# Block sums spread by DMA, expert 0's w2 in two loads, and one more x transposed by DMA, in a fused sparse-attention and routing kernel

## The chip, the cores and the metric

The kernel runs on one core of a Trainium2 chip. The metric is device time in microseconds (us). Before the change the median of three runs is 668.64 us (668.12 to 669.35). Five engines take part: TensorE (PE; its weight loads are listed as PEld), VectorE (DVE), ScalarE (ACT), GpSimd (POOL) and SyncE (SP). SP only issues DMAs; POOL mostly does. Each engine works through its own instructions in the order in which they were written, so an instruction that waits holds up everything behind it on that engine.

## The reference

The computation is a sparse attention whose output, with all heads side by side, is the input of a dense mixture of experts. Shapes: q, k and v are 4 batches x 8 heads x 768 positions x 64; the experts' input x is 3072 x 512; there are 8 experts with 1024 hidden units.

```python
k_sum = k.reshape(B, H, nb, 32, D).max(axis=3)      # 24 blocks of 32 keys
v_sum = v.reshape(B, H, nb, 32, D).mean(axis=3)
scores_l = where(|i - j| < 16, scale * q @ k.T, -1e9)
scores_s = scale * q @ k_sum.T + log(32)
a = softmax(concat(scores_l, scores_s))             # one softmax over both
attn = a @ concat(v, v_sum)
x = attn with heads side by side                    # (3072, 512)
P = exp(x @ w_gate - max)
repeat 8 times: P /= row sums; P /= column sums; P *= N / E
out = sum over e of P[:, e] * (relu(x @ w1[e]) @ w2[e])
```

Each query therefore sees its 31 nearest keys and, for every block of 32 keys, one summary key (the maximum) with one summary value (the mean).

## The kernel before

**Pairs.** Two heads are handled together as a "pair"; there are 16 pairs, four to a batch (`PB = 4`, `NP = 16`). For a pair, a chunk of 128 queries (there are `G = 6`) is multiplied with its 128 keys plus 16 on each side. Pairs 0 to 3 (batch 0) are done in two halves, with special code that brings the first results early. Pairs 4 to 15 are "whole" pairs, and most of the change concerns them.

**A whole pair** goes through these steps. k, q and v are loaded by POOL's DMAs, which cast from f32 to bf16 (`load_qk` L268, `load_v` L285). k and q are transposed to put the head dimension on partitions: on TensorE (`tr` L292) for pairs below `BY_DMA = 12`, by a DMA that SP issues (`tr_dma` L325) from there on. DVE takes the block maxima of k. TensorE sums v over blocks (`block_sums` L349), and DVE writes the sums into `V_e` (`block_out` L358). TensorE makes scores (`scores` L380), ACT exponentiates them, DVE masks them. `values` (L427) multiplies with v and, in a second product per chunk, with `V_e`; DVE normalizes (`normalize` L529); the result is transposed into `xT` on TensorE (`to_xT` L544, line L548) and copied out by DVE or ACT (`x_out` L551). For pairs at or above `X_BY_DMA = 12`, except the last of a batch, SP issues a DMA that transposes instead (`x_dma` L556).

**V_e** is a value buffer with one row of slots per chunk, `[128, G, 2 * 65]` in bf16. Its rows 0 to 63 hold the block sums of the pair's two heads, the same for every chunk. Its rows 64 to 127 hold the few neighbouring values on either side of each chunk, brought there by four small DMAs (`near_values` L369), issued by SP for pairs below 12 and by POOL above. In the kernel before, DVE writes the sums to chunk 0 and then copies them to the five others (L365). There are `NE = 2` such buffers, used in turn, and pair i cannot write its buffer until the value products of pair i - 2 are through. POOL fills in the constants (`value_constants` L692).

**Expert 0 in between.** While the attention runs, TensorE fills the time between its steps with expert 0: x of a batch is cut in two halves of 384 tokens, and each half takes 8 hidden products of four matmuls (`hidden0` L594, line L209) and 3 output products in two parts of four matmuls each (`project0` L605, line L214). Part 0 reads the first half of w2's rows, part 1 the second. The router's products (`logits`, line L568) need the whole of a batch's x. Experts 1 to 7 follow as one long run, in a form with fewer products per block (L762 and L813); this run is not touched.

**The order.** All of this is registered as units with a cost, dependencies and a priority, and a planner (`Plan.order` L58) plays it through with these costs and writes the instructions out, engine by engine, in the order that it found. A unit's `lag` is what the planner adds after its end before others may start; for a load it stands for the time to landing (`load` L860). The costs and lags decide only the order. What an instruction really waits for comes from what it reads and writes. POOL's loads form one chain: pair 0's q and so on down to v of pair 4 (L1051), then expert 0's w2 (L1052), then the constants of the `V_e` and `E_e` buffers (L1053 to L1055), then the loads of pair 5 onward. Up to `NQ = 6` pairs are loaded ahead.

Of the kernel before, what the change touches and what calls it, by code (L numbers as in the profile page):

```python
# [10 lines left out]
BF16 = mybir.dt.bfloat16  # L11
F16 = mybir.dt.float16
# [116 lines left out]
def kernel(  # L129
# [10 lines left out]
    nc = tc.nc  # L140
# [19 lines left out]
    BY_DMA = 12  # L160
    X_BY_DMA = 12
    WHOLE = 12
# [30 lines left out]

    def load_w2(e):
        w2s[e] = wpool.tile([128, KF, DM], F16, tag="w2", name="w2")
        nc.gpsimd.dma_start(out=w2s[e][:], in_=moe_w2[e].rearrange("(fk p) d -> p fk d", p=128))

# [21 lines left out]
    NB = PB  # L219
    NE = 2  # L220
    NS = 1
    NA = 3
    stage = ExitStack()
    with tc.manual_schedule():
# [20 lines left out]

        E_e = [attn.tile([128, G, 128], BF16, name=f"Ee{i}") for i in range(NE)]
        V_e = [attn.tile([128, G, 2 * VD], BF16, name=f"Ve{i}") for i in range(NE)]

# [109 lines left out]
        def block_out(i):  # L358
            vs = at.pop(("vs", i))[0:64, :].rearrange("p (j d) -> p j d", j=2)
            dst = V_s[i][0:64, :] if i < PB else V_e[i % NE][0:64, 0, :]  # L360
            nc.vector.tensor_tensor(out=dst.rearrange("p (j x) -> p j x", j=2)[:, :, 0:D], in0=vs,
                                    in1=own_n[:].to_broadcast([64, 2, D]), op=ALU.mult)
            if i >= PB:
                ve = V_e[i % NE]
                nc.vector.tensor_copy(out=ve[0:64, 1:G, :],  # L365
                                      in_=ve[0:64, 0:1, :].to_broadcast([64, G - 1, 2 * VD]))


        def near_values(i):  # L369

            sv, ve = v_x[i % NQ], V_e[i % NE]
            eng = nc.sync if i < BY_DMA else nc.gpsimd
            for j in range(2):
                c0, q0 = VD * j, 64 + 32 * j
                eng.dma_start(out=ve[q0 + W:q0 + 2 * W, 1:G, c0:c0 + VD],
                              in_=sv[128 - W:128, j, 0:G - 1, :])
                eng.dma_start(out=ve[q0:q0 + W, 0:G - 1, c0:c0 + VD],
                              in_=sv[0:W, j, 1:G, :])
# [48 lines left out]
        def values(i, h):  # L427
            sv, ee, ve, em = v_x[i % NQ], E_e[i % NE], V_e[i % NE], at["em", i]
            av = at["av", i, h] = bank("a", "av")
            for cc in range(HG):  # L430
                c, o = HG * h + cc, cc * 2 * VD
                for j in range(2):
                    nc.tensor.matmul(av[:, o + j * VD:o + (j + 1) * VD],  # L433
                                     lhsT=em[:, j, c, :], rhs=sv[:, j, c, :],
                                     start=(cc == 0 and j == 0), stop=False,
                                     skip_group_check=True)
            for cc in range(HG):
                c, o = HG * h + cc, cc * 2 * VD
                nc.tensor.matmul(av[:, o:o + 2 * VD], lhsT=ee[:, c, :], rhs=ve[:, c, :],  # L439
                                 start=False, stop=True, skip_group_check=True)  # L440
# [418 lines left out]

        def load(key, fn, issue, us, deps=()):  # L860
            last[0] = add("POOL", issue, fn, [last[0], *deps])
            last[1] = add("DMA", us, None, [add("RING", 0, None, [last[0]], lag=1.4 if last[1] else 0.9), last[1]], 100.0)
            U[key] = add("LAND", 0, None, [last[1]], lag=0.9)

        def load_pair(i, parts="kqv"):
            old = i - NQ
            for c in parts:
                if c == "v":
                    load(("v", i), lambda: load_v(i), 1.05, 1.85 if i < PB else 1.6,
                         [U.get(("A", old, 1)), U.get(("near", old))])  # L870
                elif i < PB and c in "qr":
                    h = "qr".index(c)
                    load(("q", i, h), lambda h=h: load_qk(i, 1, h), 0.65, 0.65)
                else:
                    z = "kq".index(c)
                    load((c, i), lambda z=z: load_qk(i, z), 0.75 if i < PB else 1.65,
                         1.2 if i < PB else 1.4, [U.get(("tr", old, z)), U.get(("tr", old, 2))])

        def pair_start(i, prio):
# [18 lines left out]
            if i >= PB:  # L898
                U["km", i] = add("DVE", 0.23, lambda: key_max_split(i), [U["ks", i]] + war_q[2:], prio)
            buf = Buffer("a")  # L900
            U["vs", i] = add("PE", 0.4, lambda: block_sums(i),
                             [U["v", i]] + ([U.get(("A", i - NE, 1)), U["vc", i % NE]] if i >= PB else []), prio + 0.01, opens=[buf])
            sc = add("DVE", 0.25, lambda: summary_constants(i), [], prio - 1.0) if 0 < i < PB else None
            U["Vs", i] = add("DVE", 0.28 if i < PB else 0.7, lambda: block_out(i), [U["vs", i], sc],
                             prio + 0.01, uses=[buf])
# [36 lines left out]
        def pair_whole(i, prio):  # L942
            U["near", i] = add("SP" if i < BY_DMA else "POOL", 2.4 if i < BY_DMA else 3.0, lambda: near_values(i),
                               [U["v", i], U.get(("A", i - NE, 1)), U["vc", i % NE]], prio, lag=5.0 if i < BY_DMA else 3.5)
            x1 = []
# [24 lines left out]
            for h in range(2):  # L970
                buf = Buffer("a")
                U["A", i, h] = add("PE", 0.4, lambda h=h: values(i, h),
                                   [U["mk", i, h], U["ed", i], U["sx", i, h], U["Vs", i], U["near", i]],
                                   prio, opens=[buf])
# [13 lines left out]
        def expert0(t0, xs):  # L988
            key, n = t0, len(halves)
            halves.append(key)  # L990
            pr = 1000.0 + n
            w = [U["w1", n] for n in range(4)]
            evac, old = [], [U.get(("pj", halves[n - 2], c)) for c in range(HG)] if n >= 2 else []
# [15 lines left out]
            for c in range(HG):  # L1009
                buf = Buffer("m")  # L1010
                p0 = add("PE", 0.88, lambda c=c: project0(key, c, 0), evac[0:4] + [U["w2"]],
                         pr + 0.1 + c * 0.02, opens=[buf])
                p1 = add("PE", 0.88, lambda c=c: project0(key, c, 1), evac[4:8] + [p0],
                         pr + 0.11 + c * 0.02, uses=[buf])
# [31 lines left out]
        for n in range(4):  # L1046
            load(("w1", n), lambda n=n: load_w1(0, n, 4), 0.85, 1.25)
            if n == 1:
                for i in range(PB):
                    load_pair(i, "r")  # L1050
        load_pair(PB, "kqv")  # L1051
        load("w2", lambda: load_w2(0), 0.85, 4.0)  # L1052
        for n in range(NE):  # L1053
            U["vc", n] = last[0] = add("POOL", 1.2, lambda n=n: value_constants(n), [last[0]])
            U["ec", n] = last[0] = add("POOL", 0.7, lambda n=n: edge_constants(n), [last[0]])  # L1055
# [36 lines left out]
        def transposed():  # L1092
# [4 lines left out]
            if X_BY_DMA < NP:  # L1097
                nc.gpsimd.tensor_copy(out=warm[:, 4:5], in_=xT[0:32, PB - 2, (B - 1) * S:(B - 1) * S + 1])
            ve = V_e[(NP - 1) % NE]
            for j in range(2):  # L1100
                nc.gpsimd.tensor_copy(out=warm[:, 2 + j:3 + j],
                                      in_=ve[64 + 32 * j:96 + 32 * j, G - 2, VD * j:VD * j + 1])

        last[0] = add("POOL", 0.3, transposed, [last[0], U["near", NP - 1]] + [U["kT", NP - 1, z] for z in range(2)]
                      + [U["x", i] for i in range(X_BY_DMA, NP - 1)])
# [211 lines left out]
```

The softmax here doesn't subtract the row's maximum and nothing guards it: scores larger than these inputs give would overflow.

## Time and profile before

| what | us |
|---|---|
| median of three runs | 668.64 |
| the profiled execution | 668.44 |
| its span, first instruction to last | 666.70 |
| TensorE busy in the span | 657.9 |
| DVE busy | 549.2 |
| ACT busy | 410.5 |
| POOL busy | 198.3 |
| DVE copies of block sums to five chunks (L365), 12 of 0.483 | 5.8 |
| TensorE transposes of x (L548) in the whole span | 78 instructions |
| w2 of expert 0, from issue to landing | 10.49 |

The profile is one execution on the chip. A row for a group of instructions names the line, the engine, the operation, and what it writes and reads ("out<-in"), followed by the count and the times. A timeline row starts with the start in us from the span's start and the duration; a bracket at the end gives the engine's idle time just before and what ended it. A row for DMA issues gives the count, the size of one and the median time from issue to landing. The granted TensorE clock is full throughout the span.

### The profile page before, as it was taken

Reading aid. Unit: us, or ns where it says so; the run is one execution under the profiler, and the core shown is the slowest. Engines: PE = TensorE matmul, PEld = TensorE weight load, DVE = VectorE, ACT = ScalarE, POOL = GpSimd, SP = SyncE. Lnnn points to the kernel's source line nnn. Section 1 sums busy time; section 2 is a strip of 40 time slices with the busy share of each in tenths; the row PEclk is TensorE's granted clock in tenths of the full one; section 3 lists DMA queues with packets and bytes.
Section 4 is the critical chain, followed back from the end, with each engine's and each line's share of the span. In section 5 each row is a group of like instructions: output and inputs, shape, how many; then the busy total and the mean of one; then the engine's idle time right before and its main releaser. Section 6 shows DMA issues by size and latency. Waiting matters only on the chain.

```text
span 666.7 us, 13260 instructions
## 1 busy us (share of the span) xinstructions
PE 657.9 (99%) x5132; PEld 434.0 (65%) x5132; DVE 549.2 (82%) x1035; ACT 410.5 (62%) x768; POOL 198.3 (30%) x256
## 2 busy tenths in 40 slices
PE   8999999999999999999999999999999999999996
PEld 4656665555676666666666666666666666666665
DVE  7889978799989787888789887888778877988776
ACT  6767766555986566556565665656665656556652
POOL 8899622100132222222221222222122213222123
PEclk9999999999999999999999999999999999999999
DMA  9999992700863647473654656373837465334656
GB/s 168 165 149 145 132 88 43 127 0 1 137 112 64 117 75 116 79 127 64 98 102 76 123 83 106 65 127 61 130 64 130 77 95 95 64 64 112 159 134 198
DMA packets 112542, 67.89 MB, mean 102 GB/s; under 512 B 77920, under 2 KB 90464, under 8 KB 112480
## 3 DMA queue, kind: packets, MB, share of 16 engines
q0 software_dynamic: 94800, 57.46, 65.7%
q1 hardware_dynamic: 17152, 9.58, 6.5%
q8 instruction: 40, 0.66, 0.4%
q14 instruction: 22, 0.18, 0.1%
q10 hardware_dynamic: 528, 0.02, 0.0%
HBM read 52.45 MB, written 6.29 MB: 88 GB/s over the span
## 4 chain that ended last, share of the span: by engine, by line
PE 94%; DMA 3%; POOL 2%; issue 0%; DVE 0%; ACT 0%; POOLq 0%; DVEq 0%
PE yps L813 22%; PE pA L762 22%; PE pY L813 17%; PE pQ L762 11%; PE yps L214 6%; PE hps L209 6%; PE pR L762 5%; DMA w<-in_moe_w_dram 3%; PE sg L345 1%; PE tkq L301 1%; PE av L433 1%; PE vs L355 1%; PE av L439 1%; POOL vx L287 1%; PE tx L548 1%; PE ss L459 1%
## 5 line engine op out<-in xcount | busy, mean ns | idle before, releaser
L813 PEld LDWEIGHTS <-h 128*128 128x128 f16 x2352 | 230.1, 98 | 89.3 <-issue 1.0
L841 POOL DMA_DIRECT2D out_acc<-y x120 | 101.5, 880 | 372.0 <-ACT y L837 97.8
L837 ACT ACTIVATE y<-pY,P_sb 128x256 f32<-128x256 f32 x168 | 79.8, 476 | 124.2 <-PE pY L813 122.5
L828 DVE SCALAR_TENSOR_TENSOR out_acc<-yps,P_sb,out_acc 128x512 f32<-128x512 f32 x128 | 95.2, 744 | 30.2 <-PE yps L813 30.0
L796 DVE TENSOR_TENSOR h<-h 128x1024 f16<-128x1024 f16 x168 | 109.0, 684 | 1.2
L813 PE MATMUL pY<-w,h 128*128 128x256 f16 x672 | 100.2, 273 | 0.6 <-ACT y L837 0.6
L762 PE MATMUL pA<-xT,w 128*128 128x512 f16 x336 | 98.5, 379 | 0.0
L813 PE MATMUL yps<-w2sum,h 128*128 128x256 f16 x672 | 98.1, 273 | 0.0
L813 PE MATMUL yps<-w,h 128*128 128x256 f16 x672 | 93.3, 273 | 0.0
L828 DVE SCALAR_TENSOR_TENSOR out_acc<-pY,P_sb,out_acc 128x512 f32<-128x512 f32 x84 | 62.9, 748 | 29.9 <-PE pY L813 28.2
L762 PEld LDWEIGHTS <-w 128*128 128x128 f16 x672 | 65.8, 98 | 30.9 <-issue 0.2
L762 PEld LDWEIGHTS <-w1sum 128*128 128x128 f16 x504 | 49.3, 98 | 44.2
L784 DVE CUSTOM_DVE_ANT_0 h<-pQ,snap 128x512 f16<-128x512 f32 x84 | 57.6, 685 | 6.0 <-ACT snap L205 3.3
L784 DVE CUSTOM_DVE_ANT_0 h<-pA,snap 128x512 f16<-128x512 f32 x84 | 57.3, 683 | 6.0 <-PE pA L762 5.9
L200 ACT ACTIVATE h<-pA 128x512 f16<-128x512 f32 x84 | 50.6, 603 | 12.4 <-PE pA L762 12.2
L200 ACT ACTIVATE h<-pR 128x512 f16<-128x512 f32 x84 | 50.1, 596 | 7.5 <-PE pR L762 7.4
L205 ACT COPY pR<-pA 128x512 f32<-128x512 f32 x84 | 48.0, 571 | 7.4 <-PE pA L762 6.4
L813 PE MATMUL pY<-w2sum,h 128*128 128x256 f16 x336 | 50.4, 273 | 0.0
L762 PE MATMUL pA<-xsum,w 128*128 128x512 f16 x168 | 50.0, 379 | 0.0
L762 PE MATMUL pQ<-xsum,w1sum 128*128 128x512 f16 x168 | 50.0, 379 | 0.0
L762 PE MATMUL pQ<-xT,w1sum 128*128 128x512 f16 x168 | 50.0, 379 | 0.0
L762 PE MATMUL pA<-xsum,w1sum 128*128 128x512 f16 x168 | 50.0, 379 | 0.0
(149 smaller groups left out, 845.9 us busy)
## 6 DMA issues: line engine op xcount, KB each, us to landing
out_acc<-y POOLq DMA_DIRECT2D x120, 256.0 KB, 3.4
w<-in_moe_w_dram POOLq DMA_DIRECT2D x15, 1024.0 KB, 10.6
out_dram<-out_acc SPq DMA_DIRECT2D x24, 256.0 KB, 2.5
qst<-in_q_dram POOLq DMA_DIRECT2D x32, 96.0 KB, 5.8
vx<-in_v_dram POOLq DMA_DIRECT2D x15, 192.0 KB, 6.6
kst<-in_k_dram POOLq DMA_DIRECT2D x24, 96.0 KB, 6.0
w<-in_moe_w_dram POOLq DMA_DIRECT2D x4, 256.0 KB, 7.9
kst<-in_k_dram POOLq DMA_DIRECT2D x3, 192.0 KB, 4.7
```

What stands on the lines that cost most here:

```text
L200: nc.scalar.activation(out=out, in_=in_, func=AF.Relu, bias=0.0, scale=1.0)
L205: (nc.scalar.copy if eng == "ACT" else nc.vector.tensor_copy)(out=out, in_=in_)
L209: nc.tensor.matmul(hp[:, 0:n], lhsT=w1s[e][:, dk, f * 128:(f + 1) * 128], rhs=xT[:, dk, t0:t0 + n], start=(dk == 0), stop=(dk == KD - 1))
L214: nc.tensor.matmul(yp[:, d], lhsT=h[:, f, c * 128:(c + 1) * 128], rhs=w2s[e][:, f, d], start=(f == 0), stop=(f == KF - 1))
L287: nc.gpsimd.dma_start(out=v_x[i % NQ][:].rearrange("p j g x -> p (j g) x")[:, :, 0:D], in_=v[b, h0:h0 + 2].rearrange("j (g p) d -> p (j g) ...
L762: nc.tensor.matmul(dst[:], lhsT=lhsT, rhs=rhs, start=first and k == 0, stop=k == HK - 1, skip_group_check=True)
L784: nc.vector._custom_dve(dve_ops.TENSOR_ADD_SAT, out=ring(e, p, q)[:, q % 2, blk, :], in0=at[src, e, p, q][:], in1=at.pop(("snap", n, e, p, ...
L796: nc.vector.tensor_tensor(out=h[:, :, out_, :], in0=h[:, :, a, :], in1=h[:, :, b, :], op=op)
L813: nc.tensor.matmul(dst[:, d], lhsT=lhsT, rhs=rhs, start=f == 0 and n in (1, 5, 2), stop=f == HF - 1, skip_group_check=True)
L828: nc.vector.scalar_tensor_tensor(out=o, in0=y, scalar=scalar, in1=o, op0=ALU.mult, op1=ALU.add)
L837: nc.scalar.activation(out=at[key][:, d], in_=src, func=AF.Copy, bias=0.0, scale=P_sb[:, t, e:e + 1])
L841: nc.gpsimd.dma_start(out=o, in_=at.pop(("y", e, p, c, key))[:], accum_op=ALU.add)
```

## The change

There are three parts, with the changes that they need in the planner's input:

1. Block sums: DVE writes them to chunk 0 only, and a new DMA (`spread_sums`) copies them to the five other chunks. SP issues it for pairs 4 to 11, POOL for pairs 12 to 15. `V_e` gets three buffers (`NV = 3`) where it had two; `E_e` keeps two. The value products now depend on the spread.
2. w2 of expert 0 is loaded in two halves of its rows: the first after q of pair 4, the second after v of pair 4. Each part of the output products depends on its own half.
3. `X_BY_DMA` goes from 12 to 10, so x of pair 10 is transposed by a DMA from SP. Pair 11 is the last of its batch and stays on TensorE.

The planner's lag for the landing of the loads of pairs 4 and on goes from 0.9 to 1.8 (k and q) or 2.3 (v), and for the halves of w2 it is 2.3. The constants of the third `V_e` are filled ahead of those of `E_e`.

```diff
-    X_BY_DMA = 12
+    X_BY_DMA = 10
...
-    def load_w2(e):
-        w2s[e] = wpool.tile([128, KF, DM], F16, tag="w2", name="w2")
-        nc.gpsimd.dma_start(out=w2s[e][:], in_=moe_w2[e].rearrange("(fk p) d -> p fk d", p=128))
+    def load_w2(e, part=0, parts=1):
+        if part == 0:
+            w2s[e] = wpool.tile([128, KF, DM], F16, tag="w2", name="w2")
+        fk = slice(part * KF // parts, (part + 1) * KF // parts)
+        nc.gpsimd.dma_start(out=w2s[e][:, fk, :], in_=moe_w2[e].rearrange("(fk p) d -> p fk d", p=128)[:, fk, :])
...
+    NV = 3
...
-        V_e = [attn.tile([128, G, 2 * VD], BF16, name=f"Ve{i}") for i in range(NE)]
+        V_e = [attn.tile([128, G, 2 * VD], BF16, name=f"Ve{i}") for i in range(NV)]
...
-            if i >= PB:
-                ve = V_e[i % NE]
-                nc.vector.tensor_copy(out=ve[0:64, 1:G, :],
-                                      in_=ve[0:64, 0:1, :].to_broadcast([64, G - 1, 2 * VD]))
+        def spread_sums(i):
+            ve = V_e[i % NV]
+            (nc.sync if i < BY_DMA else nc.gpsimd).dma_start(
+                out=ve[0:64, 1:G, :], in_=ve[0:64, 0:1, :].to_broadcast([64, G - 1, 2 * VD]))
...
-        def load(key, fn, issue, us, deps=()):
+        def load(key, fn, issue, us, deps=(), lag=0.9):
...
-            U[key] = add("LAND", 0, None, [last[1]], lag=0.9)
+            U[key] = add("LAND", 0, None, [last[1]], lag=lag)
...
-            U["Vs", i] = add("DVE", 0.28 if i < PB else 0.7, lambda: block_out(i), [U["vs", i], sc],
+            U["Vs", i] = add("DVE", 0.28, lambda: block_out(i), [U["vs", i], sc],
...
+            U["sp", i] = add("SP" if i < BY_DMA else "POOL", 0.62 if i < BY_DMA else 0.9, lambda: spread_sums(i), [U["Vs", i]],
+                             prio, lag=5.0 if i < BY_DMA else 3.5)
...
-                                   [U["mk", i, h], U["ed", i], U["sx", i, h], U["Vs", i], U["near", i]],
+                                   [U["mk", i, h], U["ed", i], U["sx", i, h], U["sp", i], U["near", i]],
...
-        load_pair(PB, "kqv")
-        load("w2", lambda: load_w2(0), 0.85, 4.0)
-        for n in range(NE):
+        load_pair(PB, "kq")
+        load(("w2", 0), lambda: load_w2(0, 0, 2), 0.85, 2.0, (), 2.3)
+        load_pair(PB, "v")
+        load(("w2", 1), lambda: load_w2(0, 1, 2), 0.85, 2.0, (), 2.3)
+        for n in range(NV):
             U["vc", n] = last[0] = add("POOL", 1.2, lambda n=n: value_constants(n), [last[0]])
+        for n in range(NE):
             U["ec", n] = last[0] = add("POOL", 0.7, lambda n=n: edge_constants(n), [last[0]])
```

Every other use of `V_e` goes by `NV` in place of `NE`, and the steps that must wait for a `V_e` buffer (block sums, near values) wait for the value products of pair i - 3 in place of i - 2.

## The prediction

> **What bounds the kernel now.** I began with the page's busy list, then asked the windows how TensorE fares stage by stage, because one share over 666.7 us mixes an attention stage (to about 120 us) with a long run of expert products.
>
> ```profile
> PE 657.9 (99%) x5132; PEld 434.0 (65%) x5132; DVE 549.2 (82%) x1035; ACT 410.5 (62%) x768; POOL 198.3 (30%) x256
> ...
> 20.00:40.00 20.00, 18.48 (x261) 11.68 (x261) 16.45 (x46) 13.58 (x23) 18.24 (x28) 1.00 1.80 156
> 40.00:60.00 20.00, 20.00 (x259) 13.15 (x258) 18.74 (x48) 14.25 (x23) 19.85 (x24) 1.00 2.46 146
> 60.00:80.00 20.00, 20.00 (x251) 13.08 (x250) 18.39 (x51) 15.76 (x26) 17.11 (x20) 1.00 2.47 139
> 600.00:667.00 67.00, 61.59 (x455) 44.19 (x452) 49.20 (x74) 33.62 (x66) 16.22 (x18) 1.00 0.58 150
> ```
>
> In a window row the numbers after the length are the busy time of PE, PEld, DVE, ACT and POOL. PE lacks 2.2 us in the first 20 us, 1.52 us between 20 and 40, 5.4 us in the last window (the final copies and stores; 0.4 us of it is window beyond the span's end), and nothing from 40 to 600. That nothing is real and not just overlapping bars: in the chain of waits four 512-column products of L214 take 0.86 to 0.87 us, 216 ns each, and four 384-column ones of L209 0.65 us. So any PE time saved or lost before 600 us comes out at the end one for one. What else can be won in the stretch of the change is one wait:
>
> ```profile
> engine line waited for: us in total, times, longest us
> PE yps L214 <- DMA w<-in_moe_w_dram: 1.3, 1, 1.3
> ```
>
> The timeline puts it at one place, with the loads ahead of it:
>
> ```profile
> 23.24 1.04 POOL L287 DMA_DIRECT2D vx<-in_v_dram  x1
> 24.24 0.91 POOL L196 DMA_DIRECT2D w<-in_moe_w_dram  x1
> ...
> 32.92 0.51 PE L355 MATMUL vs<-vx,m_blk 128*128 128x128 bf16 x6
> 34.77 1.02 PE L214 MATMUL yps<-w,h 128*128 128x512 f16 x4 [1.34 <-DMA w<-in_moe_w_dram]
> ```
>
> v of pair 4 lands 5.8 us after its issue (29.04) but is first multiplied at 32.92; expert 0's w2, queued behind it, lands at 34.73, 10.49 us after its issue, and PE has stood 1.34 us for it. The two loads stand in the wrong order for PE, by about 4 us of slack.
>
> Last, the DMA issues, for what a new transfer will take:
>
> ```profile
> Ve<-vx SPq DMA_DIRECT2D x32, 10.2 KB, 5.4
> Ve<-vx POOLq DMA_DIRECT2D x16, 10.2 KB, 3.1
> kT<-kst SPq DMA_TRANSPOSE x4, 7.8
> qT<-qst SPq DMA_TRANSPOSE x4, 8.5
> xT<-xs SPq DMA_TRANSPOSE x3, 3.4
> ```
>
> The last number is the median from issue to landing. 10 KB takes 5.4 us beside the loads, and as little as 1.7 us once they are over; transposes take 7.8 and 8.5 us between 66 and 94 us, 3.4 us after 102.
>
> **What the Trainium skill says.** "DMA: Bandwidth & Descriptors", section "Issuing engines are not separate DMA queues": DMAs from SP and POOL share the same 16 engines and interleave. The 5.4 against 1.7 us agree: SP's small copies are slow only while POOL's loads run. The same page, "Specifications", asks for at least 512 B a piece for line rate; the spread moves pieces of 260 B. No run yet shows its price. "Perfetto Trace Analysis", "Identifying the Most-Contended Engine", warns that PE's busy share doesn't measure its headroom; hence the check by start-to-start times above.
>
> **The change, part by part.**
>
> *w2 in two loads.* New POOL order: k, q of pair 4, first half of w2, v, second half. The q of pair 4 landed at 26.89 and v at 29.04, so v took 2.15 us of the queue, and w2 34.73 - 29.04 = 5.69. In the new order I estimate: half w2 at 26.89 + 2.85 = 29.7, v at 31.9, the rest at 34.7. The first three projections (part 0, L1011) need only the first half and come to PE at about 33.3, 3.6 us later than it. They are 3 x 0.87 = 2.6 us of work that fills the hole until the second half is there. Gain: 1.34 us. Pair 4's block sums (32.92) still find v, now with 1.0 us to spare instead of 3.9. SP's four copies of its near values (L375, L377; first issue 29.13, 2.7 us in all) move to 31.9, landing by about 40; its value products stood at 40.51. No net cost while other PE work is at hand.
>
> *POOL's queue.* One more load issue (0.9 us) and the constants of a third V_e (0.74 + 0.20 + 0.09 + 0.09, with gaps 1.3 us) stand ahead of k of pair 5: 2.2 us later issue. Its old issue at 29.21 waited in the DMA queue behind w2 anyway (landed 35.2 and 36.2), so I take about 0.7 us on the landing, 2.2 at worst. The transposes stood at 37.07. The rows of later pairs show 2.4 to 5 us between landing and first use, so the shift dies out there.
>
> *Spread by DMA.* Off DVE: 12 copies of 64x650 at 483 ns = 5.8 us. DVE isn't the bound, but at 18.74 of 20 us it sets the attention's pace, so this is cover for other parts and I book it at nothing. In its place 12 DMAs of 64 x 5 pieces: 83 KB each, 8 on SP (0.6 us of issue, as a near copy), 4 on POOL (0.52). Price on the DMA engines, from the page's second queue: 17152 packets took 6.5% of 16 x 666.7 us, 40 ns each; 320 x 40 ns / 16 = 0.8 us per spread (an estimate; 0.4 to 1.6). Latency on the path from block sums to values: 5.4 us for 0.48. The gap between these two on PE was 7.6 and 7.4 us for pairs 4 and 5 and 11 to 13 us for pairs 6 to 11 (70.48 to 83.26 for pair 10). A spread costs Vs (0.9 us after the products), 2.5 us of near issues ahead of it, 0.6 and 5.4: 9.4 us, or 7 when the near copies went first, which the third buffer allows one pair sooner. So 6 to 11 are covered; 4 and 5 slip by 0 to 2 us, behind expert 0's products. On POOL pairs 12 to 15 have 8 us and more, with 3.1 us landings.
>
> *x of pair 10 by DMA.* Six transposes leave PE: 52.34 to 52.67 for another pair, 0.33 to 0.34 us. A copy of 0.55 us leaves DVE (or 0.8 ACT). SP gets one transpose (1.2 us issue), the DMA engines 768 packets, x 40 / 16 = 1.9 us.
>
> Sum on PE: -1.34 - 0.34 = -1.68 us. Profiled span 666.70 - 1.68 = 665.02. The profiled execution took 668.44 in all, 1.74 beyond its span and 0.20 under the median; the same difference on the median gives 668.64 - 1.68 = 666.96.
>
> **Rivals.** About 0.2% (1.34 us) is what this kernel's measurement tells from no change.
>
> *Given back in the attention stage (same).* Expert 0's products are the filler, and the filler is finite: the last projection of batch 0 is at 66.86, and batch 1's first hidden product at 68.69 needs x of pair 7, copied by 66.95. If PE arrives 1.34 us early but pairs 4 to 7 don't, it waits here, 0 to 1.3 us; late spreads or a late k of pair 5 add 0 to 2. Against: DVE sheds 4 x 0.48 = 1.9 us by then, and pair 8's work can go ahead. Price: -0.34 to +1 net, centre 668.2.
>
> *x of pair 10 comes late (slower).* Its value products end at 84.0, normalize at 85.3; SP is free at 84.3. The planner counts on 1.5 + 1.7 + 2.0 = 5.2 us to landing; transposes there took 7.8 to 8.5, at most 9.4. The router's products of batch 2 (L568) stood at 93.09, 7.8 us after normalize: a usual landing makes PE wait 0 to 0.7 us, 9.4 makes 1.6. All PE work stands behind that wait. The new traffic between 64 and 92 (three spreads at 0.8, 1.9 for the transpose itself) can add up to 4 us. It decides from a wait of 1.68 + 1.34 = 3.0 us, a landing 10.8 us after issue. With 5 us of wait: 668.64 - 1.68 + 5 = 672; centre 671. The planner may have placed L568 later, which excludes the wait.
>
> *More than the sum (faster still).* Each step from score products (64-row weights) to full products costs 0.1 us or so (0.76 for 0.65 at L209); a new order with ten fewer of them gives 1 us more: 666.0.
>
> **How the numbers follow.** Forecast 0.45 (its own range 666.4 to 667.3); given back 0.28; late x or another wait of that size 0.19; more than the sum 0.08. Faster is the first and the last, less a little of the first at its edge: 0.51. Same is most of "given back": 0.26. Slower, 0.23: the late x, and the part of "given back" where pairs 4 and 5 lose over 3 us. Range: 665.9 holds most of "more than the sum", 670.9 half of the slower case.
>
> **What would show it.** The wait of L214 for w is gone and its first projection runs near 33.3; between 40 and 600 us PE stays full; six fewer transposes at L548 (72 for 78), no 64x650 copy on DVE. Wrong would be: a PE wait at L439 for the V_e landing (pairs 4 and 5), at L568 or L209 for x by DMA, or at L209 about 66 us for x of pair 7; or the w wait still there for its second half.

## The result, and the profile after

The changed kernel takes 677.0 us (median of six runs, 674.6 to 678.2) where the kernel before takes 668.4 beside it: a ratio of 1.0129, 95% interval 1.0108 to 1.0151. It is 8.6 us slower. The profiled execution took 677.49 us, and its span is 675.3 us, 8.6 us longer than before.

The line of busy times from the page, and the windows of the attention stage (after the length: busy time of PE, PEld, DVE, ACT, POOL; then the granted clock):

```profile
PE 659.7 (98%) x5126; PEld 435.6 (64%) x5126; DVE 544.6 (81%) x1021; ACT 412.2 (61%) x769; POOL 203.4 (30%) x265
...
20.00:40.00 20.00, 19.88 (x275) 12.51 (x275) 17.18 (x45) 13.93 (x24) 19.37 (x32) 1.00 1.73 157
40.00:60.00 20.00, 20.00 (x260) 13.60 (x256) 17.23 (x50) 16.28 (x27) 20.00 (x24) 1.00 2.27 157
60.00:80.00 20.00, 18.77 (x254) 12.99 (x252) 16.77 (x46) 16.07 (x26) 16.50 (x20) 1.00 2.19 145
80.00:100.00 20.00, 13.39 (x120) 7.66 (x118) 12.01 (x34) 8.71 (x17) 9.02 (x16) 0.83 1.43 120
```

The last window in the kernel before:

```profile
80.00:100.00 20.00, 20.00 (x198) 11.47 (x196) 16.49 (x45) 11.84 (x24) 4.27 (x8) 1.00 1.05 93
```

Between 20 and 40 us PE has won 1.4 us (19.88 for 18.48), as forecast. It loses 1.2 us between 60 and 80 and 6.6 us between 80 and 100, where before it stood nowhere. The last column but two shows a second loss: the clock is 0.83 in that window. The waits name the cause; the columns are the total, the number and the longest:

```profile
engine line waited for: us in total, times, longest us
PE av L444 <- DMA Ve<-vx: 5.8, 1, 5.8
PE av L444 <- DMA Ve<-Ve: 2.0, 2, 1.2
```

L444 is the value product with `V_e` (L439 before). It waits for pair 12's near values, then for its spread, and once, at 61.72 us, for the spread of pair 7. The timeline at the long wait:

```profile
90.54 0.35 PE L438 MATMUL av<-vx,em 128*128 128x65 bf16 x6
96.69 0.27 PE L444 MATMUL av<-Ve,Ee 128*128 128x130 bf16 x1 [5.80 <-DMA Ve<-vx]
97.76 0.38 PE L444 MATMUL av<-Ve,Ee 128*128 128x130 bf16 x2 [0.80 <-DMA Ve<-Ve]
...
99.18 2.74 PE L211 MATMUL hps<-xT,w 128*128 128x384 f16 x8
```

The last line is the aftermath: eight hidden products take 2.74 us, where eight took 1.46 at 89.24 us, before the stall. Windows of 2 us show the granted clock, which is the first number after PE's count:

```profile
92.00:94.00 2.00, 0.00 (x0) 0.83 1.36 104
98.00:100.00 2.00, 2.00 (x16) 0.50 0.37 57
102.00:104.00 2.00, 2.00 (x28) 0.61 0.93 152
104.00:106.00 2.00, 2.00 (x26) 1.00 0.00 0
```

A mean of 0.61 between 102 and 104 puts the return to full clock near 103.6. From 97.8 to there half of 5.8 us is lost, 2.9. The account is then 7.8 us of waits at L444, 2.9 of half clock, less 1.34 (wait for w2) and 0.34 (six transposes): 9.0, against 8.6 found in the span.

What the transfers took from issue to landing between 64 and 92 us:

```profile
Ve<-vx POOLq DMA_DIRECT2D x5, 10.2 KB, 9.8
...
Ve<-Ve POOLq DMA_DIRECT2D x1, 81.2 KB, 7.9
...
kT<-kst SPq DMA_TRANSPOSE x4, 9.5
```

The prediction had 3.1 us for the first, from the whole span, and 5.4 us for a spread. These rows give medians; when a single transfer landed is also in the trace, and is given in the text from here on. The near values of pair 12 were issued from 82.40 on and landed by 96.55; before, they were issued from 84.44 and landed by 93.45. v of pair 15 landed at 95.46, for 90.78 before. So near values whose issue began 2.0 us earlier landed 3.1 us later, and PE asked for them 8.8 us earlier than before: it came to the value products of pair 12 at 90.54 for 99.33. In the kernel before, the one with `V_e` then passed without a wait:

```profile
99.52 0.34 PE L439 MATMUL av<-Ve,Ee 128*128 128x130 bf16 x3
```

That gives two suspects, which may need each other. **Order:** DVE is relieved and there is a third buffer, so the planner, whose lags for landing are fixed numbers (5.0 us on SP, 3.5 on POOL), puts pair 12 earlier than its data can be there. In its own clock the products of pair 12 moved from 98.7 to 90.2 us. **Traffic:** 83 KB a pair in 260 B pieces make loads, transposes and near values land later.

### The profile page after: what moved, and what is told of

It reads as the page before. It is cut to its first block, busy times and chain, and to the rows that moved or that the text cites. A ratio compares the mean times of both kernels' runs of the same rounds, so it can differ in the third digit from the quotient of the medians.

```text
span 675.3 us, 13268 instructions
## 1 busy us (share of the span) xinstructions
PE 659.7 (98%) x5126; PEld 435.6 (64%) x5126; DVE 544.6 (81%) x1021; ACT 412.2 (61%) x769; POOL 203.4 (30%) x265
## 4 chain that ended last, share of the span: by engine, by line
PE 91%; DMA 7%; DVE 1%; issue 0%; SPq 0%; ACT 0%; DVEq 0%
PE yps L818 22%; PE pA L767 21%; PE pY L818 16%; PE pQ L767 11%; PE pR L767 5%; PE hps L211 5%; PE yps L216 5%; DMA Ve<-Ve 2%; DMA qst<-in_q_dram 2%; DMA vx<-in_v_dram 1%; DMA kvf<-in_v_dram 1%; PE sg L348 1%; DMA Ve<-vx 1%; PE av L515 1%; PE vs L358 1%; PE av L444 0%
## 5 line engine op out<-in xcount | busy, mean ns | idle before, releaser
L207 ACT COPY pR<-pA 128x512 f32<-128x512 f32 x81 | 46.2, 570 | 9.6 <-PE pA L767 8.9
L211 PE MATMUL hps<-xT,w 128*128 128x384 f16 x256 | 50.2, 334 | 0.0
L767 PE MATMUL pR<-xT,w 128*128 128x512 f16 x168 | 50.0, 379 | 0.0
```

The source lines that it names most:

```text
L207: (nc.scalar.copy if eng == "ACT" else nc.vector.tensor_copy)(out=out, in_=in_)
L211: nc.tensor.matmul(hp[:, 0:n], lhsT=w1s[e][:, dk, f * 128:(f + 1) * 128], rhs=xT[:, dk, t0:t0 + n], start=(dk == 0), stop=(dk == KD - 1))
L767: nc.tensor.matmul(dst[:], lhsT=lhsT, rhs=rhs, start=first and k == 0, stop=k == HK - 1, skip_group_check=True)
```

## The experiments

In each, the ratio is to the kernel before on the same chip, with its 95% interval.

### The parts that are not the spread

**e1.** The kernel before with the two loads of w2 and the new load lags, and nothing else.

```diff
-        load_pair(PB, "kqv")
-        load("w2", lambda: load_w2(0), 0.85, 4.0)
+        load_pair(PB, "kq")
+        load(("w2", 0), lambda: load_w2(0, 0, 2), 0.85, 2.0, (), 2.3)
+        load_pair(PB, "v")
+        load(("w2", 1), lambda: load_w2(0, 1, 2), 0.85, 2.0, (), 2.3)
```

> The kernel before with only w2 in two loads around v of pair 4, and the planner's lags for loads; sums on DVE, two value buffers, pair 10's x on TensorE. The sum of the prediction for this part (the 1.34 us wait of L214 goes, nothing replaces it): 668.4 - 1.3 = 667.1 us, ratio about 0.998, no wait of TensorE for w. Rival (the time won is given back at the end of batch 0's filler, near 66 us): 668.0 to 668.5 with a new wait at the hidden products. If this part had a share in the 8.6 us loss: over 669.

Measured: 667.43 us for 667.43, ratio 0.9998 (0.9989 to 1.0008). The wait for w is gone from its profile, whose span is 665.3 us, and the time hasn't moved.

**e5.** The kernel before once more, to see whether that wait is in another execution.

```diff
+# again
```

> The kernel before, unchanged but for a comment at its end. Theory (the 1.34 us wait for w2 belonged to one execution: with loads that land 2 us sooner it isn't there): ratio 1.000, and this profile has a wait for w2 at L214 of under 0.7 us, with w2 landed by about 33.5 us. Rival (the wait is in every execution, and the two halves paid it back elsewhere): the wait is again 1.1 to 1.6 us with w2 landing at 34.3 to 35.

Measured: 1.0003 (0.9994 to 1.0013). My theory falls: the wait is there again (0.88 us, w2 landed at 34.81), and it is there a third time in the profile of e8, 1.29 us with w2 at 34.94.

```profile
34.86 1.02 PE L214 MATMUL yps<-w,h 128*128 128x512 f16 x4 [0.88 <-DMA w<-in_moe_w_dram]
```

So the profiles gain what the prediction said, and the timed runs don't. The single times say something about why. On e1's chip 60 runs of the kernel before lie between 666.66 and 671.07, 30 of them under 667.4; of e1's 20 runs 18 lie between 667.06 and 667.79. The new order takes away most of the long runs of before, and the shortest too. The profiled executions of before have spans of 666.7 and 666.8 us; 50 of those 60 runs have shorter ones, down to 664.9. Probably w2 is in time in those. No trace shows such a run, so this is argued only. By the medians e1 does shorten the span, by 0.25 us (665.5 for 665.75), and what a run takes outside its span grows by 0.2 us (1.94 for 1.73).

**e4.** The changed kernel with DVE's copy back in place of the spread, planned so; third buffer, w2 in two loads and x of pair 10 by DMA stay.

```diff
+            if i >= FROM:
+                ve = V_e[i % NV]
+                nc.vector.tensor_copy(out=ve[0:64, 1:G, :],
+                                      in_=ve[0:64, 0:1, :].to_broadcast([64, G - 1, 2 * VD]))
...
-            U["Vs", i] = add("DVE", 0.28, lambda: block_out(i), [U["vs", i], sc],
+            U["Vs", i] = add("DVE", 0.28 if i < FROM else 0.7, lambda: block_out(i), [U["vs", i], sc],
...
-            U["sp", i] = add("SP" if i < BY_DMA else "POOL", 0.62 if i < BY_DMA else 0.9, lambda: spread_sums(i), [U["Vs", i]],
+            U["sp", i] = U["Vs", i] if i >= FROM else add("SP" if i < BY_DMA else "POOL", 0.62 if i < BY_DMA else 0.9, lambda: spread_sums(i), [U["Vs", i]],
```

The first lines stand at the end of `block_out`. Here `FROM = 4`: all whole pairs.

> The changed kernel with the block sums spread by DVE copies again (no spread DMA at all), three value buffers kept, x of pair 10 by DMA. Theory A (order): the planner puts pair 12's value products at 99.6 here, long after the near values landed, so no long wait and 667 to 669 (less the cost of a late router product, if any). Theory B (traffic): 8 spreads of an estimated 0.8 us less before 92 us, the landings of pair 12's near values come back from 96.6 to 91 to 94, also no wait. A theory in which the third buffer itself costs time expects 672 or more.

Measured: 667.68 us, 1.0005 (0.9991 to 1.0018), span 665.4, no wait at L444. The whole loss comes with the spread; the other parts together are worth nothing that can be measured.

### Order put right, spreads kept

**e2.** The changed kernel with x of pair 10 transposed by PE again.

```diff
-    X_BY_DMA = 10
+    X_BY_DMA = 12
```

> The changed kernel with pair 10's x transposed on TensorE again. Theory A (order: the planner believes that POOL's small copies for pair 12 land 3.5 us after their issue, and puts pair 12's value products 9 us earlier than before): the planner's own clock puts them at 96.2 here, at 90.2 in the changed kernel, so the 6.6 us wait falls below 2 us and the time to 668 to 670. Theory B (traffic: the extra DMAs make everything land later): one transpose of 1.9 us less, so the wait falls by about 2 us, 673 to 675.

Measured: 669.79 us, 1.0044 (1.0027 to 1.0061), and no stall between 80 and 100 us. This isn't because the transfers came sooner: near values of pair 12 landed at 96.28 and its spread at 96.52, as late as in the changed kernel (96.55 and 97.62). But the planner, with six transposes and a copy more to place, asks for them at 97.6 us. What x by DMA added was the earlier request, not later transfers.

**e3.** The changed kernel, planned with a lag of 16 us for POOL's near values and spreads.

```diff
-    prio, lag=5.0 if i < BY_DMA else 3.5)
+    prio, lag=5.0 if i < BY_DMA else 16.0)
```

> The changed kernel with the same instructions and DMAs; only the planner's lag for POOL's near values and spreads is 16 us, not 3.5, so it orders the value products of pairs 12 to 15 later. Theory A (order): the long wait at L444 for the near values and the spread of pair 12 goes, TensorE keeps its full clock, time 667 to 669. Theory B (traffic): the landings are as late as before and the work behind them comes late anyway, 673 or more.

Measured: 670.97 us, 1.0045 (1.0028 to 1.0061). The transfers land even later (near values 100.34, spread 100.78); the products come at 100.78, without a wait, at full clock. There remain a wait of 2.0 us at L211 (DVE was held 3.3 us by a transposed k) and 1.7 us for a spread on SP.

**e10.** The changed kernel, with only the lag of transposes lengthened.

```diff
-                    U["kT", i, z] = add("DMA", 1.7, None, [U["tr", i, z]], prio, lag=2.0)
+                    U["kT", i, z] = add("DMA", 1.7, None, [U["tr", i, z]], prio, lag=7.0)
```

The same was done for x of pair 10.

> The changed kernel with one number of the planner altered: a transpose of q, k or of x of pair 10 counts as landed 7 us after its transfer in place of 2. Spreads by DMA and their lags (5.0 and 3.5 us) stay. The planner puts value products of pair 12 at 95.0 us for 90.2 and of pairs 4 to 11 about as before. Theory (order is the cause, whichever lag puts it right): no stall of over 2 us at 85 to 100 us, ratio 1.003 to 1.006. Rival (only the lag of near values and spreads matters): the stall at L444 for pair 12 stays at 4 us or more, ratio 1.009 or over.

Measured: 671.21 us, 1.0046 (1.0032 to 1.0061). The stall is gone:

```profile
96.65 0.53 PE L444 MATMUL av<-Ve,Ee 128*128 128x130 bf16 x3 [0.19 <-DVE ks L336]
```

The spread of pair 12 landed at 96.77 us all the same. This profiled execution (669.42 us) is among the fastest of its eleven; three of them have a mean clock of 0.996 or less, against two of the 41 runs of before on that chip, so some may still hold a longer stall. Three unlike edits that move the request to 96 us or later take two thirds of the loss away, and each leaves about 0.45%.

### Is it one queue, or one buffer?

**e6.** The changed kernel, with near values and spreads of pairs 12 to 15 issued by SP like the others.

```diff
-            eng = nc.sync if i < BY_DMA else nc.gpsimd
+            eng = nc.sync
```

The same edit is made in `spread_sums`, and in the planner's entries for both.

> The changed kernel, with near values and spreads of pairs 12 to 15 issued by SP as those of 4 to 11 are; the planned order stays (value products of pair 12 planned at 90.2 us). Theory (POOL's queue: those five transfers were late since POOL first had the loads up to pair 15 to issue, and each of its issues waited for the landing of the one eight before): pair 12's transfers land before 93 us, PE waits at L444 for pair 12 under 2 us in place of 6.6, time 670 to 672, ratio 1.003 to 1.006. Rival (the DMA engines are simply full between 75 and 97 us, whoever issues): the landing stays at 95 us or later and the wait at 4 us or more, ratio 1.010 or over.

Measured: 672.67 us, 1.0072 (1.0057 to 1.0088). Pair 12 lands by 89.83 and PE waits 0.3 us for it. But the stall comes back at 92 us, as a wait for DVE's queue, which a late transposed k holds up:

```profile
95.67 0.80 PE L573 MATMUL lp<-wg_bf,xT 128*128 128x8 f16 x24 [3.42 <-DVE xs L546]
```

In DVE's timeline the maxima of that k (L336) waited 4.74 us for their transpose, and the normalizing of pair 12 stood behind them. POOL's queue decides who is late. It isn't the cause.

**e7.** The changed kernel with two value buffers.

```diff
-    NV = 3
+    NV = 2
```

> The changed kernel with two value buffers in place of three, so that near values of a pair again wait for the value products two pairs back; spread by DMA, two loads of w2 and x of pair 10 by DMA stay. The planner then puts pair 12's value products at 94.2 us, for 90.2. Theory (the third buffer let the planner pull pair 12 forward on a landing it had too short): about half of the stall at 90 to 97 us goes, PE waits for pair 12 1 to 4 us, ratio 1.004 to 1.009. Rival (the third buffer is what protects the long latency of the spread; without it pairs wait more): ratio over 1.013, with waits at L444 also between 40 and 90 us.

Measured: 675.7 us, 1.0120 (1.0099 to 1.0142). Here neither side was right. Without the third buffer there is a stall of 5.4 us all the same, for a transposed k that took 13.3 us to land; the planner had asked for pair 12 only 4 us later than with three. Near values of pair 12 landed at 97.56, as late as with three. The third buffer is neither cause nor protection.

**e11.** The changed kernel with lags of 7 us on SP and 16 on POOL for near values and spreads, and x of pair 10 on PE.

```diff
-    prio, lag=5.0 if i < BY_DMA else 3.5)
+    prio, lag=7.0 if i < BY_DMA else 16.0)
-    X_BY_DMA = 10
+    X_BY_DMA = 12
```

> The changed kernel with near values and spreads planned to land 7 us after issue on SP and 16 on POOL (for 5.0 and 3.5), and x of pair 10 transposed by PE again. Value products of pair 12 are planned at 97.1 us. Theory (what was left at 1.0045 was spreads on SP that the order asked for 1 to 2 us too soon, plus their traffic): waits at L444 under 0.5 us in all, ratio 1.000 to 1.003. Rival (the traffic is the rest): waits move to loads or transposes, ratio 1.004 or over.

Measured: 672.01 us, 1.0072 (1.0042 to 1.0102), against my theory. No product waits at L444, and PE waits 3.40 us elsewhere, for DVE, which this holds up:

```profile
78.80 0.95 DVE L336 TENSOR_REDUCE ks<-kT 128x24 bf16<-128x768 bf16 x1 [4.43 <-DMA kT<-kst]
```

The planner had that k at 75.4 us. Putting one link's lag right moves the wait to the next link whose lag is too short.

**e12.** The changed kernel with the four spreads on POOL, pairs 12 to 15, done by DVE: the edit of e4 with `FROM = 12`.

> The changed kernel with the spreads of pairs 12 to 15, those on POOL, done by DVE; pairs 4 to 11 are spread by DMA on SP, x of pair 10 by DMA. Value products of pair 12 are planned at 94.1 us, their scores at 82.0 us as in the changed kernel. Theory (order): near values of pair 12 land at 93 to 96 us, PE stands 0 to 3 us there, ratio 1.003 to 1.008. Rival (POOL's four spreads are the loss): ratio 1.002 or less, with no wait of over 0.7 us after 75 us.

Measured: 671.03 us, 1.0049 (1.0033 to 1.0064). The near values of pair 12, small copies that the change doesn't touch, landed between 98.1 and 98.9 us, and PE waits for them:

```profile
99.03 0.34 PE L448 MATMUL av<-Ve,Ee 128*128 128x130 bf16 x3 [2.25 <-DMA Ve<-vx]
```

With eight spreads on SP and none on POOL, POOL's transfers are still late. What comes late isn't only the spread: transfers that the change leaves alone are late with it.

### Order and traffic apart, and together

**e8.** Traffic alone: the kernel before in its own order, with one unread copy a pair, 0.8 of a spread.

```diff
+        def unread_copy(i):
+            ve = V_e[i % NE]
+            (nc.sync if i < BY_DMA else nc.gpsimd).dma_start(
+                out=gh[i % 2][0:64], in_=ve[0:64, 0:1, :].to_broadcast([64, G - 2, 2 * VD]))
```

> The kernel before, order of work unchanged, with one more DMA a pair for pairs 4 to 15: 64 partitions x 4 pieces of 260 B (66.6 KB, 0.8 of a spread) copied from the value buffer into a tile that nobody reads, so that no product waits for it. Theory (what is left of the loss once order is put right is the wait for the spread itself, not its traffic): ratio 0.999 to 1.002, near values land at most 1 us later. Rival (the traffic of the spreads and SP's and POOL's longer queues make loads, transposes and near values late): ratio 1.003 to 1.006, with waits at L439 or L209 that the kernel before doesn't have.

Measured: 668.73 us, 1.0021 (1.0010 to 1.0032), just above my range for it. Near values of pair 12 land by 94.08 (93.45 and 94.38 in the two profiles of the kernel before) and are used at 99.88; no new wait. v of pair 15 lands at 92.86, against 90.78 and 91.87: 1.0 to 2.1 us later.

**e9.** Order alone: the changed kernel in its planned order, but DVE spreads the sums behind the planner's back and no spread DMA is issued.

```diff
+            if i >= PB:
+                ve = V_e[i % NV]
+                nc.vector.tensor_copy(out=ve[0:64, 1:G, :], in_=ve[0:64, 0:1, :].to_broadcast([64, G - 1, 2 * VD]))
...
         def spread_sums(i):
-            ve = V_e[i % NV]
-            (nc.sync if i < BY_DMA else nc.gpsimd).dma_start(
-                out=ve[0:64, 1:G, :], in_=ve[0:64, 0:1, :].to_broadcast([64, G - 1, 2 * VD]))
+            pass
```

> The changed kernel in its own order of work on every engine, planned exactly as before (third buffer, lags, two loads of w2, x of pair 10 by DMA), but the sums are spread by a copy on DVE behind each product with own_n; the 12 spread DMAs aren't issued. So it has the order without the traffic of the spreads. Theory (the order is the cause: with DVE relieved the planner asks for pair 12 at 90 us, before the near values and transposes that hang on the last loads can be there): PE still stands 3 to 6 us between 85 and 100 us, for the near values of pair 12 at L444 or a transposed k, ratio 1.006 to 1.012. Rival (the traffic of the spreads makes the rest late): near values of pair 12 land by 92 us, PE stands under 1.5 us there, ratio 1.003 or less.

Measured: 668.44 us, 1.0019 (1.0006 to 1.0033), so my theory of the order as the only cause falls. Near values of pair 12 land at 89.03 us, and the products pass without a wait:

```profile
91.97 0.41 PE L444 MATMUL av<-Ve,Ee 128*128 128x130 bf16 x3
```

What the spreads did to the rest shows in the same rows as above, 64 to 92 us, without them:

```profile
Ve<-vx POOLq DMA_DIRECT2D x12, 10.2 KB, 5.4
...
kT<-kst SPq DMA_TRANSPOSE x4, 6.0
```

These were 9.8 and 9.5 us. v of pair 15 landed at 87.85 us, for 95.46 in the same order with spreads (95.56 when the change ran again, e15).

Each suspect alone costs 0.2% (the traffic at 0.8 of its size), both together 1.3%. The last three runs ask whether it takes the two together.

**e13.** The changed kernel in its order, with two of the five pieces spread by DMA and three by DVE.

```diff
+                nc.vector.tensor_copy(out=ve[0:64, 3:G, :],
+                                      in_=ve[0:64, 0:1, :].to_broadcast([64, G - 3, 2 * VD]))
...
-                out=ve[0:64, 1:G, :], in_=ve[0:64, 0:1, :].to_broadcast([64, G - 1, 2 * VD]))
+                out=ve[0:64, 1:3, :], in_=ve[0:64, 0:1, :].to_broadcast([64, 2, 2 * VD]))
```

> The changed kernel in its own planned order, but each spread is shared: two of the five pieces a partition go by the DMA, DVE copies the other three. So 0.4 of the traffic of the spreads, in the same order. Theory (loss is early order times traffic: stall is the landing of pair 12's transfers, later by some 7.5 us for the whole traffic, less the moment the order asks, 91 to 92 us): pair 12's transfers land at 91.5 to 93.5 us, PE stands 0 to 2 us there, ratio 1.002 to 1.006. Rival (it is the waiting for the spread itself, whatever its size, that costs): the stall stays at 4 us or more, ratio 1.009 or over.

Measured: 670.59 us, 1.0042 (1.0026 to 1.0059). The ratio is as the theory has it. In the profile the stall is larger than I expected of 0.4 of the traffic, with near values landing at 94.39 us. That execution took 673.76 us, 3.2 over the median, so the usual stall will be shorter:

```profile
94.53 0.59 PE L447 MATMUL av<-Ve,Ee 128*128 128x130 bf16 x3 [4.84 <-DMA Ve<-vx]
```

**e14.** Order and unread traffic: e9 with an unread copy of 0.6 of a spread where the spread would be. DVE spreads the sums, and no product waits for the copy.

```diff
         def spread_sums(i):
-            pass
+            ve, p = V_e[i % NV], 64 * (i % 2)
+            (nc.sync if i < BY_DMA else nc.gpsimd).dma_start(
+                out=gh[p:p + 64], in_=ve[0:64, 0:1, :].to_broadcast([64, 3, 2 * VD]))
```

> The kernel of the order alone (DVE spreads the sums, 1.0019) with one unread DMA a pair in the place of each spread: 64 partitions x 3 pieces of 260 B into a tile that no one reads, 0.6 of a spread. No product waits for these copies. Theory (early order times traffic): near values of pair 12 land at 92.5 to 95 us for 89.0 without them, PE stands 1 to 4 us at L444 for them, ratio 1.004 to 1.009. Rival (traffic doesn't matter as long as nobody waits for it): they land before 91 us, ratio within 0.002 of the order alone.

Measured: 676.87 us, 1.0111 (1.0066 to 1.0156). This decides between waiting for the spread and its traffic. No product waits for these copies, and nearly the whole loss is there, at the same place:

```profile
99.26 0.58 PE L448 MATMUL av<-Ve,Ee 128*128 128x130 bf16 x3 [7.53 <-DMA Ve<-vx]
```

The near values that it waits for are the small copies of the kernel before. They were issued from 85.45 us and landed by 99.13, 10 us later than in e9, whose program differs only in the unread copies (one profile of each). The mere number of DMAs isn't it: e13 has the same twelve as the change, with 0.4 of the bytes, and a third of the loss (1.0042 for e15's 1.0135 on the same chip). Bytes and pieces of 260 B go together in all these runs, so what the size of the pieces costs wasn't tested.

**e15.** The change again, on the chip of e13 and e14.

```diff
+# again
```

> The changed kernel, unchanged but for a comment at its end, on the chip of the other two. Theory: near values and spread of pair 12 land at 95 to 98 us, PE stands 5 to 8 us in all at L444 between 85 and 100 us and its clock falls after it, ratio 1.011 to 1.015. Rival (the stall of 5.8 us belonged to one execution): the stall is under 4 us in this profile and the ratio under 1.010.

Measured: 677.45 us, 1.0135 (1.0106 to 1.0165), with the stall in the same place:

```profile
PE av L444 <- DMA Ve<-vx: 5.1, 1, 5.1
PE av L444 <- DMA Ve<-Ve: 1.8, 2, 1.5
```

## Why the prediction was wrong

Forecast were 667.0 us and a range of 665.9 to 670.9; measured are 677.0.

**The step that failed** is in the spread by DMA: "On POOL pairs 12 to 15 have 8 us and more, with 3.1 us landings." The 8 us were there: the block sums of pair 12 ran on PE at 77.83, and PE came to its value products at 90.54, 12.7 us later. But the spread landed at 97.62. POOL issued it only at 89.73, behind near values whose own issues had waited for the landings of earlier loads, and then it took 7.9 us. Three things were left out.

*The landing.* The 3.1 us is the median of 16 copies over the whole span, and most of those are issued when the loads are over. Pair 12's are issued behind the last loads. The row of the kernel before for 64 to 92 us alone would have shown 5.5 us:

```profile
Ve<-vx POOLq DMA_DIRECT2D x8, 10.2 KB, 5.5
```

With the spreads these took 9.8, and pair 12's from 8.5 to 13.4. (The 1.7 us that the prediction holds against 5.4 is of copies from POOL. SP issued none without loads about in the kernel before; in e6 it did, and they landed in 1.9.)

*The traffic.* The prediction used its 0.8 us a spread only in the rival on x of pair 10, for three spreads, and nowhere added the spreads up for the landing of the last loads and of what queues behind these. v of pair 15 lands 7.6 us later with them than without in the same order. Eight had landed by then, which makes 0.95 us each. That this is close to 0.8 is luck: for the bytes of one spread, e13 gives 1.6 us by the same measure, e14 2.1, and e8, in the order of before, 0.16 to 0.33.

*The order.* Of DVE's 5.8 us the prediction says "this is cover for other parts and I book it at nothing". But with DVE relieved the planner asked for pair 12 8.8 us sooner; x of pair 10 and the third buffer have a share in that (planned at 90.2 us, at 96.2 in e2, at 94.2 in e7). Before, near values of pair 12 had 6.1 us to spare (93.45 to 99.52). In the new order without the traffic they still landed in time, 89.03 for a request at 91.97. With it they land 7.5 us later, at 96.55, and the wait is 5.8.

The two don't simply add up. 7.5 us would have been too much for the old order's 6.1 us as well, but there the unread copies of e8, 0.8 of the traffic, hardly moved the near values (94.08, for 93.45 and 94.38). So transfers come that late only when the traffic meets the new order. A part of how can be read from the trace. Between 66 and 100 us POOL started no DMA sooner than 0.28 us after the landing of the one that it had issued eight before, so a late landing becomes a late issue. v of pair 15 was issued at 80.91 us, when the k issued eight before it had landed at 80.38; in e9 it was issued at 76.56. These 4.35 us are over half of the 7.6. Why the lag builds up in one order and hardly in the other isn't shown.

The prediction named the sign to look for, a wait at L439 for `V_e`, but for pairs 4 and 5, where none came; pair 7, counted as covered, waited 1.2 us. It also missed what a stall of that length costs on top, 2.9 us of half clock.

**w2 in two loads.** The mechanism was right: the first half landed at 28.81 us (29.7 estimated), the first part-0 projection ran on it at 31.48 (33.3 forecast), and the wait is gone.

```profile
22.29 0.78 POOL L198 DMA_DIRECT2D w<-in_moe_w_dram  x1
23.03 1.05 POOL L290 DMA_DIRECT2D vx<-in_v_dram  x1
24.04 0.80 POOL L198 DMA_DIRECT2D w<-in_moe_w_dram  x1
...
31.48 1.03 PE L216 MATMUL yps<-w,h 128*128 128x512 f16 x4
```

Its term was mis-sized: 1.34 us forecast, 0 measured (0.9998, 0.7 us either way). The prediction took a wait of the profiled execution for one of every timed run. Three profiles of before have it; that most timed runs don't is argued above, not shown.

**x of pair 10.** 72 transposes for 78, as forecast; the 0.34 us is under what can be measured. The rival that it would come late fell: it took 9.2 us to land, close to the 9.4 at worst, and in no run did the trace put a wait of the router's product down to it. The harm it did, 1.0129 for 1.0044, came through the planned order, which no rival had.

**POOL's queue.** The constants of a third buffer showed no cost: in e4, which keeps them, all parts but the spread give 1.0005.

**The rivals.** "Given back" and "more than the sum" both fell. The slower one had the right sign and mechanism, transfers that come late behind new traffic and everything on PE behind that wait, but at the wrong transfer, and at 5 us where it came to 8.6.

**What stays open.** The delay isn't in proportion to the bytes. Measured by v of pair 15 in one order, it is 5.1 us for 0.4 of the traffic (e13), 10.1 for 0.6 (e14) and 7.6 for all of it, from one profile each; two profiles of one kernel differ by 0.1 us there (change) and 1.1 (before). The 0.45% that stay in e2, e3 and e10 are larger than the 0.2% of e8. Spreads on SP that land up to 1.7 us late are seen in the profiles, but by the medians the spans of e2 and e10 are 1.7 and 3.0 us longer than before, so the rest wasn't pinned down. Some of all these ratios lies outside the span: that part has a median of 1.73 us in the kernel before, 2.17 in the changed kernel, 2.33 in e2 and 2.06 in e9, so it makes up 0.3 of the 0.7 us of "order alone". The prediction carried it over unchanged; what it depends on wasn't looked for. A planner with every lag at its measured value wasn't tried. No version beat the kernel before.

## What to carry to other kernels

A transfer has two prices: its own latency, and what it adds to the landing of everything queued with it. Take both from the stretch concerned and not from the whole run, and hold them against the spare time there. Don't take the second for a constant: here much the same copies delayed the last load by 1.0 to 2.1 us in one order of work and by 7.6 in another. And where a planner writes the order, taking work off an engine moves every request forward, while the planner's fixed landing times stay: ask which data the earlier request will find missing.

## What I had not expected of the hardware

A long stall has an aftermath. After waits of 2.25 us (e12) and 1.99 us (e3) the granted clock stayed at 1.00. With waits of 3.40 us (e11) and 3.42 us (e6) it fell to 0.50, as with 4.84, 5.80 and 7.53. It came back to 1.00 between 3.7 us (e11) and 6.9 us (the changed kernel) after PE had resumed. The Trainium skill says so: "TensorE: Matmul & The Clock Gate", section "What's actually happening", gives an idle window of about 3.4 us after which the clock is at 4/8. These runs agree, and the stretches at half clock last 3.41 us (e11), 6.83 (e6, e13, e14) or 10.24 (the changed kernel), one, two or three times the same length. But one long wait isn't the only way there: in e12 the clock was also 0.50 from 19.96 to 23.37 us, after waits of only 0.62 and 0.66, with PE busy for 2.08 of the 3.41 us before. A stall of 5.8 us on a full TensorE was worth nearly 9 us here.

Small copies of 10 KB, which land in 1.7 us once the loads are over, took up to 15.2 us behind them (e15, issued at 80.95 and landed at 96.13). POOL, which issues both, stood between these issues for landings of earlier loads; four of pair 12's five issues in the changed kernel waited 1.0 to 1.6 us so.
